# Attention prologue: the first head's operands are loaded twice and cast in place, the second head's are split on GpSimd

## The chip, the cores and the metric

One core of a Trainium2 chip runs the whole kernel. TensorE (PE) multiplies, VectorE (DVE), ScalarE (ACT) and GpSimd (POOL) work on elements, SyncE (SP) issues most DMAs. The metric is the device time of one execution in microseconds, the median of several runs; lower is better.

## The reference

The input has B = 2 batches of 8 heads, S = 768 positions, D = 64. The attention is clustered: a query sees a key only where both have the same nearest centroid of 16.

```python
q_assign = np.argmax(np.einsum('bhsd,hcd->bhsc', q_n, c_n), axis=-1)
k_assign = np.argmax(np.einsum('bhsd,hcd->bhsc', k_n, c_n), axis=-1)
mask = q_assign[:, :, :, None] == k_assign[:, :, None, :]
scores = np.where(mask, scale * np.matmul(q, k.transpose(0, 1, 3, 2)), -1e9)
attn = softmax(scores)          # over the keys
x = np.matmul(attn, v)          # then heads side by side: 1536 x 512
h = x @ w_in;  x = (h * sigmoid(h)) @ w_out
x = (sigmoid(x @ w_gate) * (x @ w_val)) @ w_out2
```

## The kernel before

Heads are worked on in pairs: a pair p has two heads j = 0 and 1, whose 64 features lie in partitions 0 to 63 (L) and 64 to 127 (U) of the tiles qq and kk. There are eight pairs, and each has 12 tiles of 128 queries (6 for each head). A tile takes scores (TensorE, L467), a row maximum (VectorE, L475), the exponential (ScalarE, L480), transposes of it (L495, L506) and, every third tile, the product with the values (L514). After the eight pairs come the two MLPs, which this change does not touch.

Scores are kept to float32 accuracy by splitting q and k into a high part in the short type fp32r and the rest. The operand qa of head j holds the high part of q in one half of the partitions and the low part in the other; ka holds the high part of k in both halves; qm and km hold the high q against the low k in one half and, in the other, 16 mask rows, one for each cluster. A mask row of a query is -2^100 at all clusters but its own, so that keys of other clusters drop out.

To find the clusters, product_of_clusters (L151) multiplies the centroids cc with qq and kk, scaled (L276) multiplies by one over each centroid's norm, similarities (L164) transposes the result so that positions lie in partitions, ranked (L169) finds the best centroid, and first_choice (L310) makes one-hot rows oh. choice_rows (L323) transposes these back, and query_rows (L326) and key_rows (L334) write them into qm and km.

For pairs 1 to 7 this is prep (L382): GpSimd scales qq in place and makes the splits, and SyncE copies the halves inside SBUF (L402 to L407), then the mask rows (L454, L455). Pieces of it are put between the tiles of the pair before (PIECES, L642). With pair 1 the cluster products come in the fourth tile of pair 0; they use the scaled qq.

Pair 0 has its own code, the prologue, from L186 to L617. In it the order on TensorE, VectorE, ScalarE and SyncE is the order in which the code is written; only GpSimd's is left to the planner, which goes by its own estimate of times, under the constraints issue_after. qq and kk are loaded in one DMA each (L199, L200); ScalarE and VectorE make the splits of both heads at once (L283 to L286); SyncE then copies halves with nine DMAs (L289 to L294) and loads vv (L295); load(1) (L133) brings qq, kk and vv of pair 1, whose qq and kk share their buffers with those of pair 0. warm(n) puts n products of a zero tile on TensorE as fillers; WARM = (10, 1, 8, 5) counts them: before the cluster products, behind them, behind the similarities, and at the end. GpSimd zeroes the unused halves of qm, km and oh (zeros, L236), for pair 1 behind `late` (L358), the low part of the second head's k.

After the prologue only TensorE's order is fixed by hand (steady, L667), until the MLPs, which again fix only TensorE's. ring (L486 in the old code's tile pool, tag "ph") holds the transposed exponentials and is idle until the first transposes.

Of the kernel before, what the change touches and what calls it, by code (L numbers as in the profile page):

```python
# [10 lines left out]
F32 = mybir.dt.float32  # L11
# [3 lines left out]
AF = mybir.ActivationFunctionType  # L15
# [11 lines left out]
SIGN = -0x80000000  # L27
WARM = (10, 1, 8, 5)


@with_exitstack
def clustered_attention_then_two_mlps(ctx, tc, qT, kT, v, cen, cenT, w1i, w1o, w2g, w2v, w2o, out):
    nc = tc.nc
    B, HP, _, S = qT.shape
    D = cen.shape[2]
    H = 2 * HP
    C = cenT.shape[3]
    P = 128
# [23 lines left out]
    def cast(eng, o, i):  # L62
        if eng is nc.scalar:
            return nc.scalar.activation(o, i, AF.Copy)  # L64
        if eng is nc.gpsimd:
            return nc.gpsimd.tensor_scalar(o, i, 1.0, 1.0, op0=ALU.mult, op1=ALU.mult)
        return nc.vector.tensor_copy(o, i)  # L67
# [41 lines left out]
    with ExitStack() as att:  # L109
# [40 lines left out]

        def product_of_clusters(pm, p, q, k):  # L151

            for h in range(2):
                for n, t in enumerate((q, k)):
                    r = slice(32 * (2 * h + n), 32 * (2 * h + n + 1))
                    nc.tensor.matmul(
                        pm[r, 0:HS].rearrange("p (i c) -> p i c", c=P),
                        lhsT=cc[:, p % HP].rearrange("p j c -> p (j c)"),
                        rhs=t.rearrange("p (i h c) -> p h i c", h=2, c=P)[:, h],
                        start=True,  # L160
                        stop=True,
                    )
# [30 lines left out]
        nc.vector.memset(cc, 0.0)  # L193
        for j, r in enumerate((L, U)):
            act_dma(cc[r, :, j], cenT[j])
        qq = raw.tile([P, S], F32, tag="qq", name="qq0")
        kk = raw.tile([P, S], F32, tag="kk", name="kk0")
        vv = hd[0].tile([P, 2, NT, D], F32, tag="vv", name="vv0")
        dma(qq, qT[0, 0])  # L199
        dma(kk, kT[0, 0])  # L200

# [62 lines left out]
        unit = cp.tile([P, HP], F32, tag="unit", name="unit")  # L264
        nc.vector.tensor_reduce(n2, csq, axis=AX.X, op=ALU.add)
        nc.scalar.activation(identb, ident, AF.Copy)
        nc.scalar.activation(r0, n2, AF.Sqrt)
# [14 lines left out]
        qh, ql, kh = (st.tile([P, S], R32, tag=t, name=f"{t}0") for t in ("qh", "ql", "kh"))  # L282
        nc.scalar.activation(qh, qq, AF.Copy, scale=scale)  # L283
        nc.vector.scalar_tensor_tensor(ql, qq, scale, qh, op0=ALU.mult, op1=ALU.subtract)
        cast(nc.scalar, kh, kk)
        nc.vector.tensor_tensor(km[L, 0], kk[L], kh[L], op=ALU.subtract)  # L286

        for j, (r, o) in enumerate(((L, U), (U, L))):
            dma(qa[r, j].bitcast(F32), qh[r].bitcast(F32))  # L289
            dma(ka[L, j].bitcast(F32), kh[r].bitcast(F32))  # L290
            dma(ka[U, j].bitcast(F32), kh[r].bitcast(F32))
            dma(qa[o, j].bitcast(F32), ql[r].bitcast(F32))
            if j:
                dma(qm[r, j].bitcast(F32), qh[r].bitcast(F32))  # L294
        dma(vv, v[0, 0])  # L295

        pm = ps_s.tile([P, 512], F32, tag="s", name="pm0")
        product_of_clusters(pm, 0, qq, kk)
        warm(WARM[1])
        sim = wk.tile([P, NT, 2, 2, C], F32, tag="sim", name="sim0", bufs=1)  # L300
        sums = sim.rearrange("p t n j c -> p (t n j c)")
        scaled(0, sums, pm[:, 0:HS])
        nc.scalar.activation(qm[L, 0], qq[L], AF.Copy, scale=scale)
        ps = ps_t.tile([P, 512], F32, tag="t", name="ps0")
        similarities(ps, sums)
        warm(WARM[2])

        chosen = []

        def first_choice(j, seen):  # L310
            sg = seen.rearrange("p (w j c) -> p j w c", j=2, c=C)[:, j]
            wq, mw = yield from ranked(0, j, sg, 2 * NT)
            if j == 0:
                chosen.append(mw)
            for n in range(2):
# [34 lines left out]
        for _ in first_choice(0, ps[:, 0:HS]):  # L350
            pass
        cast(nc.scalar, sums, ps[:, 0:HS])
        ex = sm.tile([P, 1], F32, tag="ex", name="ex", bufs=1)
        nc.scalar.activation(ex, unit[:, 0:1], AF.Exp)
        mine = sm.tile([P, 2 * NT], F32, tag="mine", name="mine", bufs=1)
        with tc.issue_after(cast(nc.gpsimd, mine, chosen.pop()).ins):
            with tc.issue_after(zeros(0, 1).ins):
                late = nc.gpsimd.tensor_tensor(km[U, 1], kk[U], kh[U], op=ALU.subtract)  # L358
        half = NT // 2
        pts = [ps_t.tile([P, 1024], BF16, tag="t", name=f"pt0_0{n}") for n in range(2)]  # L360
        choice_rows(pts[1], 0, 0, half)
        for n in range(2):
            for i in range(half):
                choice_rows(pts[n], 0, n * half + i, i)
        query_rows(0, pts[1], half, 0, 1)
        chosen.append(key_rows(nc.vector, 0, pts[0], 0, 0, half))
        key_rows(nc.scalar, 0, pts[1], 0, half, half)
        query_rows(0, pts[0], 1, 1, half - 1)
        query_rows(0, pts[1], 0, half, half)

        on_pool = {}
# [113 lines left out]

        ring = wk.tile([P, NT, S], F32, tag="ph", name="ph", bufs=1)  # L486
        shared = {}
# [655 lines left out]
def _layout(i):  # L1143
# [10 lines left out]
    def columns(w):  # L1154
# [12 lines left out]
        "cen": np.broadcast_to(cen.transpose(1, 2, 0, 3), (2, 2, *cen.shape[1:3], H // 2, D)).reshape(P, H // 2, D),  # L1167
        "cenT": cen.transpose(1, 3, 0, 2),
        "w1i": columns(i["moe_w_in"]),
# [25 lines left out]
```

## Time and profile before

| | |
|---|---|
| median of 3 runs | 775.22 us (774.85 to 776.21) |
| the profiled execution | 775.89 us, of which the span from the first to the last instruction is 774.2 |
| TensorE busy | 761.2 us (98%) |
| VectorE, ScalarE, GpSimd busy | 623.7, 403.1, 393.4 us |
| DMA | 71.60 MB, mean 92 GB/s |

Busy time of TensorE counts a product until its modelled end, so it is a share of time in which products were under way, not of what the array can do. Times in the rows below are us from the start of the span.

### The profile page before, as it was taken

How to read it: one execution, taken by the hardware profiler on the slowest of the kernel's cores; microseconds unless marked ns; L12 is line 12 of the kernel's file. 1: busy time of each engine (PE TensorE's matmuls, PEld its weight loads, DVE VectorE, ACT ScalarE, POOL GpSimd, SP SyncE). 2: the span in 40 equal slices, each digit the busy share in tenths (PEclk: the TensorE clock that was granted, in tenths of full speed). 3: DMA queues.
4: the chain of work that ended last, by engine and by line, in shares of the span. 5: the costliest groups of instructions: out<-in, count | busy, mean ns of one | idle time of the engine just before them, and what ended most of it. 6: DMA issues, size and time to landing. Idle time of an engine off the chain costs nothing.

```text
span 774.2 us, 11459 instructions
## 1 busy us (share of the span) xinstructions
PE 761.2 (98%) x4313; PEld 652.5 (84%) x4314; DVE 623.7 (81%) x787; ACT 403.1 (52%) x691; POOL 393.4 (51%) x345
## 2 busy tenths in 40 slices
PE   7999999999999999999999999999999999999998
PEld 4666776677768998898989989998998989899896
DVE  7887887788797968989779669997596997979645
ACT  6777776776886662533615526546442425343120
POOL 5334134643655773755647515544573837748320
PEclk9999999999999999999999999999999999999999
DMA  7776457447122122233122111221121221121004
GB/s 214 183 198 172 113 153 194 116 126 200 35 85 70 58 82 83 82 112 100 36 80 83 54 55 55 88 78 55 36 73 55 82 83 55 55 82 55 1 0 163
DMA packets 25487, 71.60 MB, mean 92 GB/s; under 512 B 4484, under 2 KB 4952, under 8 KB 25432
## 3 DMA queue, kind: packets, MB, share of 16 engines
q1 hardware_dynamic: 24888, 70.84, 31.0%
q8 instruction: 34, 0.56, 0.3%
q14 instruction: 21, 0.17, 0.1%
q10 hardware_dynamic: 544, 0.03, 0.0%
HBM read 48.01 MB, written 3.19 MB: 66 GB/s over the span
## 4 chain that ended last, share of the span: by engine, by line
PE 86%; DVE 8%; DMA 2%; issue 1%; ACT 1%; SPq 0%; ACTq 0%; DVEq 0%
PE z L1012 12%; PE s L467 7%; PE v L514 7%; PE t L506 5%; PE y L953 4%; PE h_0w L837 3%; PE h_0x L837 3%; PE g_0w L837 3%; PE u L495 2%; PE g_0x L837 2%; PE v_0w L837 2%; PE v_0x L837 2%; PE r L903 2%; PE q L903 2%; PE y_20None L953 2%; PE y_11None L953 2%
## 5 line engine op out<-in xcount | busy, mean ns | idle before, releaser
L480 ACT ACTIVATE e<-s,nm 128x768 f32<-128x768 f32 x96 | 86.4, 900 | 26.7 <-DVE nm L475 26.5
L475 DVE TENSOR_REDUCE nm<-s 128x1 f32<-128x768 f32 x96 | 91.4, 953 | 10.8 <-PE s L467 9.8
L1012 PE MATMUL z<-wu,ghb 128*128 128x512 f32 (+1 forms) x292 | 89.6, 388 | 0.5 <-DVE acc L933 0.5
L514 PE MATMUL v<-ph,vv 128*64 128x384 f32 x384 | 69.2, 494 | 0.2 <-DVE ph L67 0.2
L1012 PEld LDWEIGHTS z<-wu,ghb 128*128 128x128 f32 x292 | 54.1, 188 | 12.5 <-issue 1.3
L467 PE MATMUL s<-ka,qa 128*128 128x384 f32 x192 | 57.7, 381 | 2.3 <-ACT e L480 1.9
L506 PE MATMUL t<-ident,e 128*128 128x128 f32 x384 | 58.4, 275 | 1.4 <-ACT ph L64 0.5
L1012 PE MATMUL z<-wu,glb 128*128 128x512 f32 (+1 forms) x146 | 57.0, 391 | 0.0
L514 PEld LDWEIGHTS v<-ph,vv 128*64 128x64 f32 x384 | 25.2, 136 | 32.8 <-issue 28.5
L64 ACT ACTIVATE ph<-t 128x512 f32<-128x512 f32 x68 | 40.6, 598 | 23.1 <-PE t L506 22.3
L467 PE MATMUL s<-k,q 128*128 128x384 f32 x192 | 49.6, 339 | 0.8 <-DMA q<-rows 0.8
L506 PEld LDWEIGHTS t<-ident,e 128*128 128x128 f32 x384 | 44.1, 140 | 4.5 <-DVE ph L67 3.6
L933 DVE TENSOR_TENSOR acc<-z,acc 128x1024 f32<-128x1024 f32 (+2 forms) x32 | 36.6, 1153 | 13.6 <-PE z L1012 13.0
L67 DVE COPY ph<-u 128x512 f32<-128x512 f32 x48 | 32.8, 683 | 18.1 <-PE u L495 18.1
L545 POOL TENSOR_TENSOR acc<-xf,rb 128x768 f32<-128x768 f32 x7 | 12.8, 1834 | 61.2 <-DMA rb<-d_rb 49.2
L495 PEld LDWEIGHTS u<-ident,e 128*128 128x128 f32 x192 | 23.4, 141 | 21.4 <-issue 18.6
L495 PE MATMUL u<-ident,e 128*128 128x128 f32 x192 | 38.5, 282 | 0.0
L734 POOL TENSOR_TENSOR wo<-co,wo 128x512 fp32r<-128x512 f32 x16 | 22.5, 1410 | 30.0 <-ACT wo L64 30.0
L467 PEld LDWEIGHTS s<-k,q 128*128 128x128 f32 x192 | 34.6, 188 | 1.3 <-DMA q<-rows 1.1
L467 PEld LDWEIGHTS s<-ka,qa 128*128 128x128 f32 x192 | 28.9, 190 | 5.5 <-ACT e L480 3.4
L1012 PEld LDWEIGHTS z<-wu,glb 128*128 128x128 f32 x146 | 27.4, 188 | 7.1 <-DVE glb L893 1.6
L953 PE MATMUL y<-gha,wo 128*128 128x384 f32 x128 | 32.8, 334 | 0.0
(627 smaller groups left out, 2125.4 us busy)
## 6 DMA issues: line engine op xcount, KB each, us to landing
ri<-in_w1i SPq DMA_DIRECT2D x16, 512.0 KB, 3.3
ro<-in_w1o SPq DMA_DIRECT2D x16, 512.0 KB, 3.3
ka<-kh SPq DMA_DIRECT2D x32, 192.0 KB, 3.6
rg<-in_w2g SPq DMA_DIRECT2D x12, 512.0 KB, 3.2
rv<-in_w2v SPq DMA_DIRECT2D x12, 512.0 KB, 3.3
ru<-in_w2o SPq DMA_DIRECT2D x12, 512.0 KB, 3.3
qq<-in_qT SPq DMA_DIRECT2D x8, 384.0 KB, 4.2
kk<-in_kT SPq DMA_DIRECT2D x8, 384.0 KB, 4.2
```

The costliest lines, as they stand in the source:

```text
L64: return nc.scalar.activation(o, i, AF.Copy)
L67: return nc.vector.tensor_copy(o, i)
L467: nc.tensor.matmul(s[:, g, 0:HS], lhsT=a[:, j, i * P : (i + 1) * P], rhs=c[:, j, g * HS : (g + 1) * HS], start=n == 0, stop=n == 1,)
L475: maxima.append(nc.vector.tensor_reduce(nm, s[:, :, 0:HS], axis=AX.XY, op=ALU.max, negate=True))
L480: x = nc.scalar.activation(e, s[:, :, 0:HS], AF.Exp, bias=nm, scale=1.0, accum_out=tots[p][:, n : n + 1])
L495: nc.tensor.transpose(both[:, kt - 4, i % 2, :], e[:, kt * P : (kt + 1) * P], ident)
L506: nc.tensor.transpose(t[:, kt, :], e[:, kt * P : (kt + 1) * P], ident)
L514: m = nc.tensor.matmul(o[(L, U)[kt % 2]], lhsT=vv[:, j, kt, :], rhs=ring[:, kt, g * G : (g + 1) * G], start=n < 2, stop=n >= NT - 2,)
L837: nc.tensor.matmul(o[:, b, 0:HS], lhsT=w[a][s][:, k, :], rhs=right[b, q][t][:, k, :], start=start and k == 0 and n == 0, stop=k == KQ - 1 ...
L933: nc.vector.tensor_tensor(z, o, z, op=ALU.add)
L953: nc.tensor.matmul(o[:, d, 0:width], lhsT=s[:, d, k, :], rhs=t[:, c], start=k == 0 and m == 0, stop=k == 1 and m == 2,)
L1012: nc.tensor.matmul(o[:, a, c], lhsT=s[:, q * P : (q + 1) * P], rhs=r[:, c], start=k == 0 and m == 0, stop=k == 1 and m == 2, skip_group_ch ...
```

## The change

The first head's rows (partitions 0 to 63 of the DRAM arrays) are loaded twice, into both halves of two slices of ring, sq0 and sk0. Casts from there write qa, ka, qm and km of head 0 where they are used, so that no DMA copies them. The second head's rows are loaded into the upper halves of qq and kk. Cluster products of head 0 use 64 rows of sq0 and sk0; head 1 has its own products, transposes and sums behind those. GpSimd scales qq[U] in place and makes kh, qh and ql of head 1, and SyncE copies these with five DMAs, issued behind the first choice. The centroids for cc come in one DMA, from which VectorE makes two copies. The ScalarE table for the exponential is loaded earlier. The fillers are 7, 1, 7 and 5.

```diff
@@ -25,7 +25,7 @@
 
 LARGEST = 122879.9921875 * 2.0**-112
 SIGN = -0x80000000
-WARM = (10, 1, 8, 5)
+WARM = (7, 1, 7, 5)
 
 
 @with_exitstack
@@ -34,7 +34,7 @@
     B, HP, _, S = qT.shape
     D = cen.shape[2]
     H = 2 * HP
-    C = cenT.shape[3]
+    C = cenT.shape[2]
     P = 128
     NT = S // P
     HS = S // 2
@@ -148,15 +148,15 @@
         heads = {}
         L, U = slice(0, D), slice(D, P)
 
-        def product_of_clusters(pm, p, q, k):
+        def product_of_clusters(pm, p, q, k, rows=slice(0, P)):
 
             for h in range(2):
                 for n, t in enumerate((q, k)):
                     r = slice(32 * (2 * h + n), 32 * (2 * h + n + 1))
                     nc.tensor.matmul(
                         pm[r, 0:HS].rearrange("p (i c) -> p i c", c=P),
-                        lhsT=cc[:, p % HP].rearrange("p j c -> p (j c)"),
-                        rhs=t.rearrange("p (i h c) -> p h i c", h=2, c=P)[:, h],
+                        lhsT=cc[rows, p % HP].rearrange("p j c -> p (j c)"),
+                        rhs=t[rows].rearrange("p (i h c) -> p h i c", h=2, c=P)[:, h],
                         start=True,
                         stop=True,
                     )
@@ -191,13 +191,18 @@
         dma(cr, cen)
         cc = cp.tile([P, HP, 2, C], F32, tag="cc", name="cc")
         nc.vector.memset(cc, 0.0)
-        for j, r in enumerate((L, U)):
-            act_dma(cc[r, :, j], cenT[j])
+        ct = cp.tile([P, HP, C], F32, tag="ct", name="ct")
+        act_dma(ct, cenT)
+        ring = wk.tile([P, NT, S], F32, tag="ph", name="ph", bufs=1)
+        staged = ring[:, 0], ring[:, 1]
+        for r in (L, U):
+            for t, a in zip(staged, (qT, kT)):
+                dma(t[r], a[0, 0][L])
         qq = raw.tile([P, S], F32, tag="qq", name="qq0")
         kk = raw.tile([P, S], F32, tag="kk", name="kk0")
         vv = hd[0].tile([P, 2, NT, D], F32, tag="vv", name="vv0")
-        dma(qq, qT[0, 0])
-        dma(kk, kT[0, 0])
+        for t, a in zip((qq, kk), (qT, kT)):
+            dma(t[U], a[0, 0][U])
 
 
         wt = fin.tile([P, S], F32, tag="rb", name="wt").bitcast(BF16)[:, 0:512]
@@ -263,6 +268,8 @@
         n2, r0, r1, r2, r3, r4 = (norm(f"r{n}") for n in range(6))
         unit = cp.tile([P, HP], F32, tag="unit", name="unit")
         nc.vector.tensor_reduce(n2, csq, axis=AX.X, op=ALU.add)
+        for j, r in enumerate((L, U)):
+            nc.vector.tensor_copy(cc[r, :, j], ct[r])
         nc.scalar.activation(identb, ident, AF.Copy)
         nc.scalar.activation(r0, n2, AF.Sqrt)
         nc.vector.tensor_scalar_max(r1, r0, 1e-30)
@@ -280,38 +287,34 @@
         qm, km = q2[0], k2[0]
         heads[0] = (qa, qm, ka, km, vv)
         qh, ql, kh = (st.tile([P, S], R32, tag=t, name=f"{t}0") for t in ("qh", "ql", "kh"))
-        nc.scalar.activation(qh, qq, AF.Copy, scale=scale)
-        nc.vector.scalar_tensor_tensor(ql, qq, scale, qh, op0=ALU.mult, op1=ALU.subtract)
-        cast(nc.scalar, kh, kk)
-        nc.vector.tensor_tensor(km[L, 0], kk[L], kh[L], op=ALU.subtract)
-
-        for j, (r, o) in enumerate(((L, U), (U, L))):
-            dma(qa[r, j].bitcast(F32), qh[r].bitcast(F32))
-            dma(ka[L, j].bitcast(F32), kh[r].bitcast(F32))
-            dma(ka[U, j].bitcast(F32), kh[r].bitcast(F32))
-            dma(qa[o, j].bitcast(F32), ql[r].bitcast(F32))
-            if j:
-                dma(qm[r, j].bitcast(F32), qh[r].bitcast(F32))
-        dma(vv, v[0, 0])
-
+        sq0, sk0 = staged
+        cast(nc.scalar, ka[L, 0], sk0[L])
+        nc.gpsimd.tensor_scalar(qm[L, 0], sq0[L], scale, 1.0, op0=ALU.mult, op1=ALU.mult)
         pm = ps_s.tile([P, 512], F32, tag="s", name="pm0")
-        product_of_clusters(pm, 0, qq, kk)
+        product_of_clusters(pm, 0, sq0, sk0, L)
         warm(WARM[1])
+        nc.vector.tensor_tensor(km[L, 0], sk0[L], ka[L, 0].bitcast(F32), op=ALU.subtract)
         sim = wk.tile([P, NT, 2, 2, C], F32, tag="sim", name="sim0", bufs=1)
         sums = sim.rearrange("p t n j c -> p (t n j c)")
         scaled(0, sums, pm[:, 0:HS])
-        nc.scalar.activation(qm[L, 0], qq[L], AF.Copy, scale=scale)
         ps = ps_t.tile([P, 512], F32, tag="t", name="ps0")
         similarities(ps, sums)
+        nc.scalar.activation(qa[:, 0], sq0, AF.Copy, scale=scale)
+        cast(nc.scalar, ka[U, 0], sk0[U])
+        pm = ps_s.tile([P, 512], F32, tag="s", name="pm0_1")
+        product_of_clusters(pm, 0, qq, kk, U)
         warm(WARM[2])
+        nc.gpsimd.tensor_scalar(qq[U], qq[U], scale, 1.0, op0=ALU.mult, op1=ALU.mult)
+        cast(nc.gpsimd, kh[U], kk[U])
+        cast(nc.gpsimd, qh[U], qq[U])
+        ex = sm.tile([P, 1], F32, tag="ex", name="ex", bufs=1)
+        nc.scalar.activation(ex, unit[:, 0:1], AF.Exp)
 
         chosen = []
 
         def first_choice(j, seen):
             sg = seen.rearrange("p (w j c) -> p j w c", j=2, c=C)[:, j]
             wq, mw = yield from ranked(0, j, sg, 2 * NT)
-            if j == 0:
-                chosen.append(mw)
             for n in range(2):
                 nc.vector.tensor_tensor(
                     oh[0][:, :, j, n, 0:C],
@@ -349,24 +352,36 @@
 
         for _ in first_choice(0, ps[:, 0:HS]):
             pass
-        cast(nc.scalar, sums, ps[:, 0:HS])
-        ex = sm.tile([P, 1], F32, tag="ex", name="ex", bufs=1)
-        nc.scalar.activation(ex, unit[:, 0:1], AF.Exp)
-        mine = sm.tile([P, 2 * NT], F32, tag="mine", name="mine", bufs=1)
-        with tc.issue_after(cast(nc.gpsimd, mine, chosen.pop()).ins):
-            with tc.issue_after(zeros(0, 1).ins):
-                late = nc.gpsimd.tensor_tensor(km[U, 1], kk[U], kh[U], op=ALU.subtract)
+        scaled(0, sums, pm[:, 0:HS])
+        lows = nc.vector.scalar_tensor_tensor(
+            qa[U, 0], sq0[U], scale, qa[U, 0].bitcast(F32), op0=ALU.mult, op1=ALU.subtract
+        )
+        with tc.issue_after(lows.ins):
+            lows = nc.gpsimd.tensor_tensor(ql[U], qq[U], qh[U], op=ALU.subtract)
+        dma(qa[U, 1].bitcast(F32), qh[U].bitcast(F32))
+        dma(ka[L, 1].bitcast(F32), kh[U].bitcast(F32))
+        dma(ka[U, 1].bitcast(F32), kh[U].bitcast(F32))
+        dma(qm[U, 1].bitcast(F32), qh[U].bitcast(F32))
+        dma(qa[L, 1].bitcast(F32), ql[U].bitcast(F32))
+        dma(vv, v[0, 0])
+        with tc.issue_after(lows.ins):
+            last = zeros(0, 1)
+        with tc.issue_after(last.ins):
+            late = nc.gpsimd.tensor_tensor(km[U, 1], kk[U], kh[U], op=ALU.subtract)
         half = NT // 2
         pts = [ps_t.tile([P, 1024], BF16, tag="t", name=f"pt0_0{n}") for n in range(2)]
         choice_rows(pts[1], 0, 0, half)
         for n in range(2):
             for i in range(half):
                 choice_rows(pts[n], 0, n * half + i, i)
+        ps = ps_t.tile([P, 512], F32, tag="t", name="ps0_1")
+        similarities(ps, sums)
         query_rows(0, pts[1], half, 0, 1)
         chosen.append(key_rows(nc.vector, 0, pts[0], 0, 0, half))
         key_rows(nc.scalar, 0, pts[1], 0, half, half)
         query_rows(0, pts[0], 1, 1, half - 1)
         query_rows(0, pts[1], 0, half, half)
+        cast(nc.scalar, sums, ps[:, 0:HS])
 
         on_pool = {}
 
@@ -483,7 +498,6 @@
             latest[:] = [x]
             prob[p, j, i] = e
 
-        ring = wk.tile([P, NT, S], F32, tag="ph", name="ph", bufs=1)
         shared = {}
 
         def transposes(p, j, i):
@@ -1165,7 +1179,7 @@
         "kT": pairs(k),
         "v": v.reshape(B, H // 2, 2, S // P, P, D).transpose(0, 1, 4, 2, 3, 5),
         "cen": np.broadcast_to(cen.transpose(1, 2, 0, 3), (2, 2, *cen.shape[1:3], H // 2, D)).reshape(P, H // 2, D),
-        "cenT": cen.transpose(1, 3, 0, 2),
+        "cenT": cen.transpose(1, 3, 0, 2).reshape(P, H // 2, -1),
         "w1i": columns(i["moe_w_in"]),
         "w1o": w1o.reshape(K // P // 2, M // P // 2, P, -1),
         "w2g": columns(i["moe2_w_gate"]),
```

## Rows read from the trace of the kernel before

**Rows 1.** TensorE's waits in the whole kernel: us in total, times, longest.
```profile
PE s L467 <- DMA q<-rows: 0.8, 1, 0.8
```

**Rows 2.** Timeline of TensorE, first 21 us: start, us, engine, line, operation.
```profile
3.86 0.15 PEld L209 LDWEIGHTS <-wt 128*128 128x128 bf16 x1 [0.28 <-issue]
4.29 0.15 PEld L209 LDWEIGHTS <-wt 128*128 128x128 bf16 x1 [0.28 <-issue]
...
5.95 0.48 PE L156 MATMUL pm<-qq,cc 128*32 128x384 f32 x1 [0.75 <-DMA cc<-in_cenT]
...
6.32 0.49 PE L156 MATMUL pm<-kk,cc 128*32 128x384 f32 x1
...
7.97 1.89 PE L209 MATMUL pw<-wt 128*128 128x512 bf16 x8
10.31 0.55 PE L324 MATMUL pt<-identb,oh 128*64 128x128 bf16 x7 [0.45 <-DVE oh L316]
...
20.65 0.48 PE L156 MATMUL pm<-qq,cc 128*32 128x384 f32 x1
```

**Rows 3.** Timeline of ScalarE in the prologue.
```profile
5.68 0.84 ACT L64 ACTIVATE kh<-kk 128x768 fp32r<-128x768 f32 x1 [0.55 <-DMA kk<-in_kT]
6.89 0.58 ACT L276 ACTIVATE sim<-pm,unit 128x384 f32<-128x384 f32 x1 [0.36 <-PE pm L156]
7.37 0.83 ACT L303 ACTIVATE q<-qq 64x768 fp32r<-64x768 f32 x1
...
9.54 1.28 ACT L354 ACT_TABLE_LOAD   x1
10.83 0.20 ACT L354 ACTIVATE ex<-unit 128x1 f32<-128x1 f32 x1
...
11.35 0.48 ACT L337 ACTIVATE k<-pt 16x384 fp32r<-16x384 bf16 x1
```

**Rows 4.** Timeline of VectorE in the prologue.
```profile
5.18 0.18 DVE L273 RECIPROCAL unit<-r 128x4 f32<-128x4 f32 x1
...
8.17 0.36 DVE L172 TENSOR_REDUCE mx<-ps 128x12 f32<-128x192 f32 x1 [0.66 <-PE ps L167]
...
9.70 0.46 DVE L316 TENSOR_TENSOR oh<-wq,mw 128x96 bf16<-128x96 bf16 x2
```

**Rows 5.** Timeline of SyncE's DMA issues: first copy, load of pair 1's kk.
```profile
5.16 0.55 SPq L289 DMA_DIRECT2D qa<-qh  x1
...
14.77 0.33 SPq L138 DMA_DIRECT2D kk<-in_kT  x1
```

**Rows 6.** Timeline of GpSimd: late, and pair 1's first operation.
```profile
11.31 1.83 POOL L358 TENSOR_TENSOR k<-kk,kh 64x768 fp32r<-64x768 f32 x1
...
19.30 0.84 POOL L394 TENSOR_SCALAR qq<-qq 128x768 f32<-128x768 f32 x1 [2.65 <-DMA qq<-in_qT]
```

**Rows 7.** Windows of the prologue; last column GB/s of all DMA.
```profile
2.00:5.00 3.00, 3.00 (x9) 0.98 (x7) 1.66 (x8) 2.49 (x5) 1.54 (x3) 1.00 0.97 306
5.50:6.00 0.50, 0.05 (x4) 0.08 (x8) 0.50 (x1) 0.32 (x1) 0.00 (x0) 1.00 0.00 0
6.00:7.50 1.50, 1.12 (x9) 0.20 (x9) 1.18 (x2) 1.14 (x3) 0.00 (x0) 1.00 0.58 131
7.50:14.50 7.00, 5.59 (x31) 3.28 (x32) 4.44 (x12) 5.30 (x11) 4.73 (x6) 1.00 0.96 217
14.50:19.50 5.00, 4.79 (x35) 4.07 (x36) 4.64 (x10) 3.58 (x8) 2.30 (x4) 1.00 0.94 304
```

**Rows 8.** Windows while two rows are broadcast from DRAM into 64 partitions each.
```profile
82.86:83.86 1.00, 1.00 (x8) 0.29 (x4) 0.93 (x3) 1.00 (x4) 0.00 (x0) 1.00 0.71 258
165.05:166.05 1.00, 1.00 (x8) 0.46 (x10) 0.97 (x2) 0.95 (x2) 0.00 (x0) 1.00 0.64 218
```

**Rows 9.** Chain of waits: pair 1's mask rows.
```profile
33.29 3.88 DMA q<-rows
```

**Rows 10.** DMA issues of the whole kernel: KB each, median us to landing.
```profile
q<-rows SPq DMA_DIRECT2D x14, 48.0 KB, 2.1
```

## The prediction

> **What bounds the kernel now.** I read the page's busy shares first, then TensorE's waits, then each engine's timeline over the first 22 us, then the DMA rates by stretch. TensorE is busy nearly all the time, so a change outside its own work can only move the moments at which it stands still. After the first tiles there is one such moment of size, 0.8 us before pair 1's first masked scores, for mask rows that come by DMA [rows 1]. The rest of the change's reach is the start. There the reader should see this chain: filler products, the cluster products at 5.95 behind a DMA (cc, though kk had landed at about 5.66), the similarities, eight fillers, the choice rows at 10.31 [rows 2]. ScalarE, with kk at 5.68, the scaled sums at 6.89 and the last key rows from 11.35 to 11.83, lets the first masked score go [rows 3]. VectorE ranks from 8.17 and has the one-hot rows at 10.16 [rows 4]. From then on the tiles run one behind another until the cluster products of pair 1 at 20.65 [rows 2].
>
> Behind this runs a second chain, easily overlooked. SyncE copies head halves in SBUF and then loads pair 1's qq and kk [rows 5]. GpSimd has zeroed all its buffers by 16.65 (19.30 less its idle 2.65) and waits until 19.30 for that qq [rows 6]. Pair 1's cluster products need GpSimd's scaled qq, so TensorE follows it with 0.51 us to spare (19.30 + 0.84 = 20.14 against 20.65). So a faster start is worth only as much as pair 1's load lets through.
>
> **First loads.** Six half loads of 197 KB (192 KiB) take the place of two of 393 KB: 1180 KB against 786 KB. Loads into 128 partitions ran at 306 GB/s; copies between 64-partition halves at 217 GB/s [rows 7]. The nearest rows to a DRAM load into 64 partitions are the later broadcasts into halves: 258 GB/s in the first microsecond, 218 in the poorest [rows 8]. I take 260, with 306 and 217 as the ends. In the sum, T is the landing of the last half, kk[U]. The old kk landed at 5.66; 786 KB at 306 GB/s is 2.57 us and 1180 KB at 260 is 4.54, so T = 5.66 - 2.57 + 4.54 = 7.63 (6.95 at 306; 8.53 at 217). The first two halves land 393/260 = 1.51 us into the same stretch, at 4.60 (4.38 to 4.90).
>
> [...]
>
> **First head, first choice.** The small cc transfers shrink to one and two VectorE copies, which I put at 0.3 us on the six small operations that end with unit at 5.36, so unit at 5.7 [rows 4]. Cluster products take 0.86 us (5.95 to 6.81), on 64 rows as on 128, since the columns are the same [rows 2]; casts likewise cost 0.83 against 0.84 us for half or all partitions [rows 3]. Products 4.65 to 5.5; scaled (0.58) to 6.3; similarities and lags as before (ranking started 0.70 us after scaled ended): ranking at 7.0; one-hot rows 1.99 us later, at 9.0 [rows 3, 4]. That is 1.2 us earlier. The km subtraction lies between unit and the ranking.
>
> **The fillers and second product take this back.** In TensorE's order the choice rows now stand behind the second head's products and seven fillers. That is T + 0.05 + 0.86 + 0.05 + 7 x 0.236 (1.89/8 [rows 2]) = T + 2.6 = 10.23, later than the one-hot rows. ScalarE is not later: 6.3, two casts of 0.84, a table load of 1.28 with a small operation of 0.2, scaled again 0.58, ends at 10.05. The old choice rows stood at 10.31, so the first masked score moves by only -0.1 us (-0.8 at 306, +0.8 at 217). The four copies that the first scores stood behind are gone; their wait lay under this chain, so it gives nothing more.
>
> **Second head on GpSimd.** qq[U] is scaled in place, so that it waits for the second product (T + 0.9). kh[U] can run in its shadow. Then scale and qh, 0.83 each: T + 2.58. SyncE's five copies stand behind qh, the first in line; vv and pair 1's loads stand behind them all. Data moved about 0.85 us after an issue (issued at 5.16, nothing until 6.0, 131 GB/s to 7.5 [rows 5, 7]). Five copies of 197 KB at 217 GB/s take 4.53: done at T + 7.98 = 15.61. The nine old ones were done at about 14.75 (1.5 us at 131 and 7 us at 217 GB/s are 1716 of their 1769 KB). So fewer copies, started later, end 0.86 us later (0.2 to 1.8), and vv and qq behind them land as much later: qq at 20.15. GpSimd is not the later one: ql 1.83, two memsets 1.4 (five took 13.14 to 16.65), late 1.83, five memsets 3.5 end at T + 11.2 = 18.9 [rows 6]. kk waits for late as its buffer's last reader, to about 15.3; it was issued at 14.77 [rows 5] and still stands behind qq's data. If GpSimd instead takes the scale before kh, all this is 0.83 us later.
>
> **The sum.** Pair 1's cluster products: 20.14 + 0.86 = 21.0 against 20.65, +0.35 (-0.3 to +1.3). The twelve copies of pair 1 start 0.86 later. The mask rows for which TensorE waits landed 3.88 us after their issue [rows 9], against a median of 2.1 in the whole kernel [rows 10]: they stood in that queue. So the end follows the queue more than TensorE; between +0.35 and +0.86 I take +0.7. The profiled execution, 775.89 (span 774.2 and 1.7 around it), would become 776.6; it lies 0.67 above the median of the runs, so against 775.22 I forecast **775.9**. All later work on TensorE is unchanged and costs nothing as long as only these waits move.
>
> **Rivals.** A measurement of this kernel tells 0.2%, 1.55 us, from no change.
> - *Halves load at the full 306 GB/s.* T = 6.95; the start gains 0.8, but the copies still end 0.2 later; the end moves by -0.3 to +0.2: 775.1. For it: 306 in the first stretch; against: 218 to 258 in rows 8. Chance 0.2.
> - *Halves at 217, or GpSimd scales before it casts.* The end moves by +1.2 to +1.8, 776.7, half of this above the bound. For it: the copies' rate [rows 7]; GpSimd's order here is the planner's. Chance 0.2. Both together, +2.4 (777.6): 0.05.
> - *Slower, by TensorE's clock.* [...] If the slow level lasted until past 10 us, the second product would cost 0.86 and the fillers 1.35 more, so choice rows at 12.4, and the kernel +2.0: 777.2. It decides only when it holds for most of the seven fillers; a delay to 8 us costs 0.4. Against it: the products from 5.95 and the gap of 0.75 before them went at the fast level. Chance 0.05.
> - *Faster.* Pair 1's loads don't hold, and the planner puts the mask rows before other traffic: -0.9 at the start and the 0.8 wait gone, -1.7: 773.5. Rows 9 and 10 show that the place in the queue matters; nothing shows that it would change. Chance 0.06.
>
> **How the numbers follow.** The likeliest case, 775.4 to 776.3, has 0.44. Low end 774.6: below the full-rate case, leaving out the faster one. High end 777.2: over the 217 rival, leaving out the doubled one and part of the clock's. Faster 0.06. Slower: half of 0.2, 0.05, 0.05, rounded to 0.2. Same 0.74.
>
> **What the profile would show.** Right: cluster products at 4.5 to 4.9, before 5.95; the second head's at 7 to 8.5, and the choice rows directly behind seven fillers, without idle time, near 10.2; VectorE's one-hot rows near 9.0; the first pair 1 qq operation on GpSimd at 19.9 to 20.5; pair 1's cluster products near 21 with an idle stretch before them, and a wait for mask rows of about 0.8 or more. Wrong: choice rows before 9.6 and pair 1's products before 20.0 (a gain not given back); idle time before choice rows (the one-hot rows bind, not the fillers); copies' data before 10.5, which would mean that the queue does not wait for qh as reckoned.

## The result, and the profile after

The changed kernel took 780.64 us (median of 5 runs, 779.32 to 781.27) against 776.21 (774.85 to 776.51) beside it: a ratio of 1.0056 with a 95% interval of 1.0043 to 1.0069. It is slower by 0.56%, where I had forecast no difference (775.9, at most 777.2). The profiled execution took 779.42, span 777.6: +3.4 on the span before. So the profile shows 3.4 of the 4.4 us that lie between the medians. Each ratio below is to the kernel before, run on the same chip.

TensorE's timeline after (start, us, operation; it answers to [rows 2]):

```profile
1.32 3.17 PE L214 MATMUL pw<-wt 128*128 128x512 bf16 x7 [1.32 <-DVE sq L232]
4.78 1.55 PE L156 MATMUL pm<-ph,cc 64*32 64x384 f32 x8 [0.29 <-DMA ph<-in_qT]
6.26 0.39 PE L214 MATMUL pw<-wt 128*128 128x512 bf16 x1
7.11 0.52 PE L167 MATMUL ps<-ident,sim 128*128 128x128 f32 x3 [0.46 <-ACT sim L283]
8.73 0.81 PE L156 MATMUL pm<-qq,cc 64*32 64x384 f32 x1 [1.10 <-DVE wq L177]
9.28 0.85 PE L156 MATMUL pm<-kk,cc 64*32 64x384 f32 x1
...
10.71 3.17 PE L214 MATMUL pw<-wt 128*128 128x512 bf16 x7
13.81 0.96 PE L327 MATMUL pt<-identb,oh 128*64 128x128 bf16 x7
...
24.54 0.48 PE L156 MATMUL pm<-qq,cc 128*32 128x384 f32 x1
```

The first head's products do start 1.2 us earlier than before, and one of them takes 0.48 to 0.60 us, about as before (0.48 to 0.51). But a product of the second head takes 0.81 to 0.85, and the seven fillers behind it take 3.17 us where eight took 1.89. The choice rows come 3.5 us later than before and pair 1's products 3.9 later. The choice rows stand directly behind the fillers, without idle time. The wait of 1.10 names VectorE's wq, which ended at about that time; in two experiments below the same product names the DMA of qq, the half that it reads.

The same stretch in windows (busy time of PE, PEld, DVE, ACT and POOL; then granted TensorE clock, DMA share, GB/s; it answers to [rows 7]):

```profile
2.00:5.00 3.00, 2.71 (x7) 0.78 (x6) 1.92 (x9) 1.05 (x4) 1.81 (x4) 1.00 0.88 220
6.00:7.50 1.50, 1.04 (x8) 0.41 (x4) 0.95 (x1) 1.42 (x3) 0.00 (x0) 1.00 1.04 207
8.50:13.50 5.00, 4.77 (x15) 1.25 (x15) 2.46 (x5) 2.13 (x4) 3.39 (x4) 0.50 0.01 2
13.50:15.00 1.50, 1.50 (x10) 1.02 (x10) 0.52 (x1) 0.14 (x1) 1.44 (x2) 0.50 0.71 160
15.30:20.00 4.70, 4.42 (x27) 3.38 (x26) 3.50 (x6) 3.45 (x9) 4.57 (x6) 1.00 1.01 235
```

Two things are to be seen. The half loads, all into the upper halves in the window from 6.0, run at 207 GB/s, near the rate of the copies in [rows 7] (217), not at 260. And the granted clock is 0.50, the lower of the two levels that these windows show, from 8.50 to 15.0; it is 0.96 between 8.00 and 8.50, so that it fell while TensorE stood idle for 1.10 us (7.63 to 8.73). The column shows 1.00 in the first microseconds too, where the seven fillers start 0.43 us apart; there the level is read from the durations. By these the clock had risen during the first head's products: the filler at 6.26 takes 0.39 and the similarities 0.52, as in the kernel before.

Not every execution went this way. Over the whole execution the mean granted clock was 0.995 and 0.996 in two of the five (779.42 and 781.27 us), and 1.00 in the other three (779.32 to 780.99). As the column reads 1.00 also where the level is low from the start, the record doesn't show what the clock did in those three.

GpSimd and SyncE's issues after ([rows 5, 6]):

```profile
4.72 0.82 POOL L292 TENSOR_SCALAR q<-ph 64x768 fp32r<-64x768 f32 x1 [1.13 <-DMA ph<-in_qT]
9.39 0.93 POOL L66 TENSOR_SCALAR kh<-kk 64x768 fp32r<-64x768 f32 x1 [3.85 <-DMA kk<-in_kT]
...
11.90 0.83 POOL L66 TENSOR_SCALAR qh<-qq 64x768 fp32r<-64x768 f32 x1
...
21.84 0.83 POOL L409 TENSOR_SCALAR qq<-qq 128x768 f32<-128x768 f32 x1 [0.36 <-DMA qq<-in_qT]
```

```profile
4.32 0.60 SPq L205 DMA_DIRECT2D kk<-in_kT  x1
12.76 0.50 SPq L361 DMA_DIRECT2D qa<-qh  x1
```

The last half, kk[U], was issued at 4.32 and landed at 9.22 (its row in the DMA issues has 4.9 us to landing). The copies wait for qh and start at 12.76, so the DMA engines move 2 GB/s from 8.5 to 13.5. TensorE's list of waits after has no row for mask rows any more; the 0.8 us of [rows 1] is gone. Pair 1's mask rows were issued 3.9 us later than before (37.20 against 33.29), as much as TensorE was late. But pair 2's loads, which stand ahead of them, were issued only 3.1 later (33.73 against 30.65), and the first rows then took 2.5 us to land, not 3.88 [rows 9].

### The profile page after: what moved, and what is told of

It is laid out like the page before. It is cut to its first block, busy times and chain, and to the rows that moved or that the text cites. A ratio compares the mean times of both kernels' runs of the same rounds, so it can differ in the third digit from the quotient of the medians.

```text
span 777.6 us, 11483 instructions
## 1 busy us (share of the span) xinstructions
PE 765.9 (98%) x4321; PEld 653.6 (84%) x4321; DVE 625.0 (80%) x789; ACT 404.0 (52%) x692; POOL 399.9 (51%) x349
## 4 chain that ended last, share of the span: by engine, by line
PE 86%; DVE 9%; issue 1%; DMA 1%; ACT 1%; POOL 0%; SPq 0%; ACTq 0%; DVEq 0%
PE z L1026 12%; PE s L482 8%; PE v L528 8%; PE t L520 5%; PE y L967 4%; PE h_0w L851 3%; PE h_0x L851 3%; PE u L509 3%; PE g_0w L851 2%; PE g_0x L851 2%; PE v_0w L851 2%; PE v_0x L851 2%; PE r L917 2%; PE q L917 2%; PE y_20None L967 2%; PE y_11None L967 2%
```

## The experiments

**Fillers before the second products, and seven fillers in the kernel before.** My first theory was that the clock, which fell after 1.10 us of idle time, made the loss, and that the place of the fillers decides it. The rival: the late second half decides.

```diff
e1_fill, on the changed kernel:
         cast(nc.scalar, ka[U, 0], sk0[U])
+        warm(7)
         pm = ps_s.tile([P, 512], F32, tag="s", name="pm0_1")
e2_before7, on the kernel before:
-WARM = (10, 1, 8, 5)
+WARM = (7, 1, 7, 5)
```

> The changed kernel with seven more fillers between the similarities of head 0 and the second head's products, so that TensorE is not idle from 7.6 to 8.7 us. If the fall of the granted clock to half (8.5 to 15.3 us) is what the late choice rows cost, and the idle stretch brings it on: the clock stays at 1.00, the second products take 0.86 us instead of 2.05 and the next seven fillers 1.65 instead of 3.1, choice rows near 11.9 instead of 13.8, and the kernel about 2 us faster than the changed one, near 778.5. If the late landing of the last half load is all that matters: choice rows at 13.5 or later and no change of time.

> The kernel before with the fillers of the change, 7, 1, 7 and 5, and nothing else. If the number of fillers at the start alone lets the clock fall: granted clock 0.50 somewhere between 5 and 15 us and 2 us or more slower. If it takes the idle stretch behind the similarities, which this kernel doesn't have: clock 1.00, choice rows at 10.3, and no difference (within 0.2%).

e1_fill: ratio 1.0064 (1.0044 to 1.0084), no better than the change. e2_before7: 1.0009 (1.0000 to 1.0018). The fillers of e1_fill, and then of e2_before7, in TensorE's timeline:

```profile
8.68 3.19 PE L214 MATMUL pw<-wt 128*128 128x512 bf16 x7
...
12.89 1.68 PE L214 MATMUL pw<-wt 128*128 128x512 bf16 x7
```

```profile
6.12 0.82 PE L156 MATMUL pm<-qq,cc 128*32 128x384 f32 x1 [1.64 <-DMA cc<-in_cenT]
...
9.11 2.39 PE L209 MATMUL pw<-wt 128*128 128x512 bf16 x7
11.49 0.55 PE L324 MATMUL pt<-identb,oh 128*64 128x128 bf16 x7
```

The cure missed: the low level held from the start until 12.3, so the new fillers only put the products off. In this execution the first head's products already took 0.82 to 0.85 us each, although the code up to them is the changed kernel's. So it does not test whether filling the gap keeps a level that has been reached. What both profiles show is that with seven fillers at the start the engine had not reached the fast level at the first products (0.82 us each instead of 0.48), in the kernel before too. In e2_before7 the choice rows came 1.2 us later than before, and the kernel lost no more than 0.2%: there is slack of about the 0.8 us for which TensorE waited anyway, and that wait is gone from its list.

**Ten and eight fillers; the second head's halves loaded earlier.**

```diff
e4_after10, on the changed kernel:
-WARM = (7, 1, 7, 5)
+WARM = (10, 1, 8, 5)
e3_order, on the changed kernel: q[U], k[U] before the upper copies
-        for r in (L, U):
-            for t, a in zip(staged, (qT, kT)):
-                dma(t[r], a[0, 0][L])
+        for t, a in zip(staged, (qT, kT)):
+            dma(t[L], a[0, 0][L])
...
+        for t, a in zip(staged, (qT, kT)):
+            dma(t[U], a[0, 0][L])
```

> The changed kernel with the fillers of the kernel before, 10, 1, 8 and 5. If the shorter first run of fillers lets the clock fall: it stays at 1.00, choice rows near 12.1 (one filler more), and 2 us faster than the changed kernel. If the idle stretch from 7.6 to 8.7 does: the clock falls at about the same time, choice rows near 14.2, and no faster than the changed kernel.

> The changed kernel with the upper halves of qq and kk loaded before the upper copies of the first head, same bytes, same fillers. If the order of the half loads sets when TensorE goes on: kk's half lands near 7.4 instead of 9.2, the second products start near 7.6 without the idle 1.1 us and at full clock, and choice rows stand near 10.2; ScalarE, which now waits for the copies (near 8.3 and 9.2), writes the last key rows near 12.9, so about 1 us slower than the kernel before. If the clock falls whatever the gap is: choice rows at 12 or later and 3 us slower than the kernel before.

e3_order: 1.0054 (1.0040 to 1.0069). GpSimd has kk[U] at 7.40 instead of 9.39, yet the low level lasts until about 13.2, the second products take 8.47 to 9.97 and the seven fillers 3.17: choice rows at 13.01. e4_after10: 1.0044 (1.0031 to 1.0057), which overlaps the changed kernel's interval; the timeline tells more. Its TensorE:

```profile
9.80 1.90 PE L214 MATMUL pw<-wt 128*128 128x512 bf16 x8
11.63 0.58 PE L327 MATMUL pt<-identb,oh 128*64 128x128 bf16 x7
...
20.09 0.61 PE L482 MATMUL s<-ka,qa 128*128 128x384 f32 x2 [1.15 <-ACT e L495]
...
23.29 0.48 PE L156 MATMUL pm<-qq,cc 128*32 128x384 f32 x1
```

The choice rows are 2.2 us earlier than in the changed kernel, with one filler more: the clock had cost about that much (kk[U] came 0.25 us earlier here). But pair 1's products are only 1.25 earlier, because of a new wait of 1.15. It goes back to VectorE (first fence), which compares beside GpSimd's `late` (second):

```profile
16.17 1.68 DVE L175 TENSOR_TENSOR eq<-sim,mx 128x192 bf16<-128x192 f32 x1
```

```profile
15.80 1.83 POOL L370 TENSOR_TENSOR k<-kk,kh 64x768 fp32r<-64x768 f32 x1
```

The comparison takes 0.36 us elsewhere, as in the kernel before at 14.48. It ends at 17.85, just after `late` (17.63).

**Half loads in the kernel before.** If loading by halves is what is slow, it must cost the kernel before too, with the same bytes.

```diff
e5_halves, on the kernel before:
-        dma(qq, qT[0, 0])
-        dma(kk, kT[0, 0])
+        for r in (L, U):
+            for t, a in zip((qq, kk), (qT, kT)):
+                dma(t[r], a[0, 0][r])
```

> The kernel before with pair 0's qq and kk loaded in four halves of 64 partitions in the order lower, lower, upper, upper; nothing else. If a load into one half runs at about 209 GB/s like the copies: kk whole near 6.9 instead of 5.66, cluster products near 7 instead of 5.95, choice rows 1.0 to 1.2 later, and about 1 us slower. If halves load at 306 GB/s: products at 6.0 and no difference.

1.0029 (1.0019 to 1.0039), 2.1 us, twice what I had expected. ScalarE has qq at 6.57 instead of 4.29, and TensorE kk at 7.44 instead of by 5.95:

```profile
6.62 0.80 PE L156 MATMUL pm<-qq,cc 128*32 128x384 f32 x2 [1.01 <-DMA qq<-in_qT]
7.44 0.48 PE L156 MATMUL pm<-kk,cc 128*32 128x384 f32 x1
```

From 3 to 5 us the DMA engines moved 259 GB/s (263, 255) where the kernel before moves 327 (325, 329); the expectation had 209 or 306. Pair 1's products stand at 22.50, 1.85 us later than before. So half loads cost this kernel 0.3% by themselves, with all its fillers and no GpSimd splits.

**`late` before the memsets; the half loads alternated.**

```diff
e6_late, on e4_after10:
         with tc.issue_after(lows.ins):
-            last = zeros(0, 1)
-        with tc.issue_after(last.ins):
             late = nc.gpsimd.tensor_tensor(km[U, 1], kk[U], kh[U], op=ALU.subtract)
+        with tc.issue_after(late.ins):
+            last = zeros(0, 1)
...
-        with tc.issue_after(late.ins):
+        with tc.issue_after(last.ins):
             zeros(1, 0)
e8_alt, on e4_after10:
-        for r in (L, U):
-            for t, a in zip(staged, (qT, kT)):
-                dma(t[r], a[0, 0][L])
...
-        for t, a in zip((qq, kk), (qT, kT)):
-            dma(t[U], a[0, 0][U])
+        for t, u, a in zip(staged, (qq, kk), (qT, kT)):
+            dma(t[L], a[0, 0][L])
+            dma(u[U], a[0, 0][U])
+        for t, a in zip(staged, (qT, kT)):
+            dma(t[U], a[0, 0][L])
```

> The changed kernel with 10, 1, 8 and 5 fillers, and the operation late on GpSimd ahead of the two memsets that stood before it, so that it no longer runs when VectorE compares sim with mx for the second head. If VectorE and GpSimd shut each other out while both read SBUF: that comparison takes 0.36 instead of 1.68 us, the tiles behind it come 1.3 us earlier, pair 1's products near 22.0 instead of 23.3, and the kernel is about 1.3 us faster than with the fillers alone (779.6), near 778.4. If the long comparison had another cause: it stays at 1.6 or more and the time at 779.6.

> The changed kernel with 10, 1, 8 and 5 fillers and the half loads in turn, lower and upper: sq0, qq, sk0, kk, then the two upper copies. If two halves together use what one alone leaves idle: near 260 GB/s or more over the first four, kk's half landed before 7.5 instead of 9.1; choice rows near 10.8 and 0.5 to 1 us faster than with the fillers alone, since ScalarE then waits for the copies. If the rate belongs to 192 KB transfers and not to the half: about 209 GB/s as before and kk's half at 7.5 or later only by its place.

e6_late: 1.0049 (1.0038 to 1.0061), no gain. The comparison falls to 0.55 us and TensorE's wait from 1.15 to 0.28, and then pair 1's products wait 0.53 us for GpSimd's scaled qq, whose load had ended 0.19 us after GpSimd was free, and then for the load of kk (the weight load, PEld, names it):

```profile
22.73 0.83 PE L156 MATMUL pm<-qq,cc 128*32 128x384 f32 x2 [0.53 <-POOL qq L409]
23.54 0.11 PEld L156 LDWEIGHTS pm<-kk,cc 128*32 128x32 f32 x1 [0.68 <-DMA kk<-in_kT]
23.55 0.51 PE L156 MATMUL pm<-kk,cc 128*32 128x384 f32 x1
```

So the comparison and the load queue are two bounds close behind one another. e8_alt: 1.0034 (1.0021 to 1.0046); kk[U] is there at 7.48, the choice rows at 11.11, but the comparison again takes 1.68 and pair 1's products start at 22.84. Its interval overlaps that of e4_after10. The gain in kk[U] is one of order: from 4 to 7 us the stream moved 241 GB/s (240, 261, 221) against 223 (209, 255, 206) in the changed kernel, far from 327. Three other profiles with the changed kernel's order of loads have 214 (e6_late), 224 (e1_fill) and 233 (e4_after10), so that alternating gave between 3 and 13%.

**Whole loads, both products together.** Whole loads of qq and kk, the two extra halves behind them, both heads' products at once, `late` first.

```diff
e7_full, on the changed kernel (the core; head 0 then takes qq[L], kk[L] for sq0[L], sk0[L]):
-WARM = (7, 1, 7, 5)
+WARM = (10, 1, 8, 5)
...
+            dma(t, a[0, 0])
+        for t, a in zip(staged, (qT, kT)):
+            dma(t[U], a[0, 0][L])
...
+        product_of_clusters(pm, 0, qq, kk, L)
+        product_of_clusters(pm1, 0, qq, kk, U)
```

> The changed kernel repaired in three places: qq and kk loaded whole first, and after them only the upper copies of the first head; both heads' products one behind the other before the similarities; 10, 1, 8 and 5 fillers and late ahead of the memsets. If half loads, idle TensorE and the shared reading are the causes: products near 5.8, choice rows near 10.4, copies of head 1 issued near 9.5, pair 1's products near 20.7, and the time within 0.15% of the kernel before. If casting in place and splitting on GpSimd cost something by themselves: 1.5 us or more slower than the kernel before.

1.0088 (1.0072 to 1.0104), the slowest of all, though both products were done at 7.96. So the second branch came: casting in place and splitting on GpSimd cost something by themselves. VectorE, GpSimd, TensorE and the windows:

```profile
11.11 1.40 DVE L319 TENSOR_TENSOR oh<-wq,mw 128x96 bf16<-128x96 bf16 x1
12.43 1.85 DVE L319 TENSOR_TENSOR oh<-wq,mw 128x96 bf16<-128x96 bf16 x1
```

```profile
10.59 1.80 POOL L360 TENSOR_TENSOR ql<-qq,qh 64x768 fp32r<-64x768 f32 x1
12.35 1.82 POOL L368 TENSOR_TENSOR k<-kk,kh 64x768 fp32r<-64x768 f32 x1
```

```profile
14.43 0.92 PE L327 MATMUL pt<-identb,oh 128*64 128x128 bf16 x7 [3.47 <-DVE oh L319]
```

```profile
14.00:20.00 6.00, 5.32 (x21) 4.30 (x23) 3.93 (x6) 3.19 (x8) 5.19 (x9) 0.50 0.96 277
20.00:21.00 1.00, 1.00 (x7) 0.76 (x5) 0.93 (x3) 0.77 (x2) 0.72 (x1) 0.92 0.87 347
```

Two one-hot operations that take 0.46 us together [rows 4] took 3.18, beside two GpSimd subtractions that ran back to back: the first ended at 12.51, just after the first subtraction (12.39), the second at 14.28, just after the second (14.17). TensorE then stood idle for 3.47 us, and its granted clock was 0.50 for the next six.

**The queue, both bounds, and the kernel before's own queue.**

```diff
e9_vv, on e8_alt: vv behind the half loads instead of behind the five copies
+        dma(vv, v[0, 0])
...
-        dma(vv, v[0, 0])
e10_both: e9_vv, with the edit of e6_late
e11_order, on the kernel before:
-        dma(vv, v[0, 0])
...
             load(1)
+            dma(vv, v[0, 0])
```

> The changed kernel with 10 and 8 fillers and the half loads alternated between the two halves of the partitions (e8_alt), and the first head pair's values vv issued straight behind the half loads instead of behind the five copies, in the time in which the DMA engines stood idle (0 GB/s from 8.5 to 13.5 us). If pair 1's loads bind, through the queue behind the copies: pair 1's kk lands about 1.3 us earlier, pair 1's cluster products stand near 21.7 instead of 22.84, and the kernel is about 1 us faster than e8_alt, +0.2% on the kernel before. If VectorE's long comparison (1.68 us at 16.17) and TensorE's own chain bind: the products stay near 22.8 and the ratio near e8_alt's +0.34%.

> e9_vv, and late (the low part of the second head's k on GpSimd) put ahead of the memsets, so that it does not run beside VectorE's comparison of pair 0. If the two are two bounds one behind the other (comparison, then loads), the comparison takes 0.6 us or less, the loads of pair 1 are early too, its cluster products stand near 21.3, and the kernel comes to within 0.15% of the kernel before. If only the queue mattered: the same as e9_vv.

> The kernel before with one edit: the load of vv is issued behind pair 1's qq and kk instead of ahead of them. If pair 1's place in the queue sets the end of the prologue, as I wrote in the prediction, pair 1's qq is scaled by GpSimd about 1.3 us earlier (near 18.0 instead of 19.30), the mask rows leave earlier and the 0.8 us wait for them shrinks: up to 0.8 us (0.1%) faster. If the queue does not bind the kernel before: no change within 0.1%, with pair 1's products still near 20.65.

e9_vv: 1.0026 (1.0016 to 1.0036). Pair 1's scale on GpSimd waits for no load, as already in e8_alt, and pair 1's products still start at 22.98: the comparison took 1.69. e10_both: 1.0022 (1.0012 to 1.0032). The comparison takes 0.36, pair 1's products start at 21.87 straight behind the scores, and GpSimd works without a pause into pair 1. VectorE and TensorE of e9_vv, then of e10_both:

```profile
15.86 1.69 DVE L175 TENSOR_TENSOR eq<-sim,mx 128x192 bf16<-128x192 f32 x1
22.98 0.48 PE L156 MATMUL pm<-qq,cc 128*32 128x384 f32 x1
```

```profile
15.80 0.36 DVE L175 TENSOR_TENSOR eq<-sim,mx 128x192 bf16<-128x192 f32 x1
21.87 0.48 PE L156 MATMUL pm<-qq,cc 128*32 128x384 f32 x1
```

In the profiles, then, `late` alone (e6_late) or the loads alone (e8_alt, e9_vv) left pair 1's products at 22.7 to 23.0, and only both brought them to 21.87. The times tell less: e9_vv and e10_both each lie below the changed kernel's interval, but e8_alt, e9_vv and e10_both overlap one another, so that neither what vv's place adds to the alternated loads nor what `late` adds to both is shown in time. e10_both did not come within 0.15%: of the expectation, the mechanism holds in the profile and the size does not. e11_order: 1.0002 (0.9994 to 1.0011). GpSimd has pair 1's qq at 18.33 instead of 19.30 and the wait for mask rows is gone, but in this execution cc came 0.7 us later [rows 2], about as much as the wait, and pair 1's products stood at 21.95. No difference can be told.

**The table load earlier.**

```diff
e12_table, on e10_both:
         nc.vector.reciprocal(unit, r4)
+        ex = sm.tile([P, 1], F32, tag="ex", name="ex", bufs=1)
+        nc.scalar.activation(ex, unit[:, 0:1], AF.Exp)
...
-        ex = sm.tile([P, 1], F32, tag="ex", name="ex", bufs=1)
-        nc.scalar.activation(ex, unit[:, 0:1], AF.Exp)
```

> e10_both, and the small exponential that loads ScalarE's table moved from between the casts of the first head and the scaled sums of the second (10.26 to 11.75 us in e10_both) to right behind the norms, where ScalarE stands idle from 4.17 to 6.29. In e10_both ScalarE lets the first masked scores go at 13.01. If what is left of the loss (+0.22%) is TensorE's chain through ScalarE, the first masked scores come at 11.8 to 12.4, pair 1's cluster products near 21.4, and the ratio falls to about +0.15%. If GpSimd, which has no idle time left ahead of pair 1's scale at 20.65, holds the rest, the scores come earlier but pair 1's products stay above 21.4 and the ratio near +0.2%.

1.0036 (1.0022 to 1.0049): a miss. ScalarE's wait goes, but the first masked scores only move from 13.01 to 12.96, now behind VectorE: the low part of qa takes 1.47 us beside a cast and a 2.41 us subtraction on GpSimd (0.96 beside a memset, in e7_full), then the key rows end at 12.81. Pair 1's products start at 21.90, as in e10_both. Most of the 2.1 us by which the span of this profile exceeds that of e10_both (776.8 against 774.7) comes later, in code that no edit touched. VectorE, GpSimd and TensorE:

```profile
50.17 2.06 DVE L436 TENSOR_TENSOR wq<-eq,mk 128x384 bf16<-128x384 bf16 x1
```

```profile
49.71 2.10 POOL L414 TENSOR_TENSOR kl<-kk,kh 128x768 fp32r<-128x768 f32 x1
```

```profile
54.46 0.66 PE L520 MATMUL t<-ident,e 128*128 128x128 f32 x4 [1.43 <-DVE ph L67]
```

The same operation, wq, takes 0.54 in e10_both and 1.04 in the kernel before. In e10_both it ran beside a cast on GpSimd (50.42 to 51.68); in the kernel before it began beside a cast that ended at 50.26, and a subtraction followed at 50.34; in e12_table it began 0.46 us behind the subtraction above and ended at 52.23, 0.42 after it. So in these three profiles its time went with where it fell against GpSimd's operations.

## Why the prediction was wrong

Two terms of the sum failed: T, the landing of the last half, and the price of the second product and its fillers, for which I took the fast level of the clock.

**First loads: mis-sized.** T was 9.22, not 7.63. By the sum's own working, 1180 KB in 9.22 - 3.09 us (5.66 - 2.57) are 192 GB/s, below even the 217 end (the bytes themselves ran at 206 to 255 a microsecond from 4 to 7, and stopped about 1 us before the landing). The 306 for whole loads was low too; from 3 to 5 us they ran at 327. The rows chosen, broadcasts from DRAM, were the wrong neighbours; the SBUF copies, also 192 KB into 64 partitions, were the right ones, and e5_halves shows the price alone. The bytes themselves moved faster than 192: the sum counts the time from the last byte to the landing as transfer.

**The fillers and second product: right in form, 3.6 us short.** I had the choice rows at T + 2.6 = 10.23; they came at 13.81. Of the 3.58, T made 1.59. The rest is the clock: from the last half to the products' end 1.55 (9.22 to 10.77) instead of 0.91, and from there 3.04 instead of 1.70, together 1.98.

**The clock rival: its price near, its chance wrong.** At the choice rows I had reckoned 2.2 us for it: 0.86 for the second product once more, and 1.35 for seven fillers at the 0.43 us between the first ones (3.86, 4.29) instead of 0.236 [rows 2]. The profile shows 1.98; in time it was not isolated, since e4_after10 overlaps the change. I gave +2.0 us and 0.05. What I held against it, that products from 5.95 ran fast, was seen behind ten fillers and says nothing of seven; e2_before7 shows the kernel before slow at that very place (0.82 us a product at 6.12, against 0.48). The way was another than I wrote: in the profiled execution the level had been reached and fell in the gap before the late half, while in e1_fill and e3_order it had not been reached. And I priced it against T = 7.63: late loads and a low clock at once, which happened, were not added up.

**VectorE beside GpSimd: left out.** The change moves five operations to GpSimd, and I asked only when GpSimd would be done with them. VectorE operations beside them grew: unit came at 5.97 instead of 5.7 because one operation on 128x4 took 0.72 us instead of 0.16 from 4.84 on, beside GpSimd's from 4.72; the low part of qa took 1.47. In the changed kernel itself this stayed off the path (ScalarE waited 3.36 us for the choice rows); with a faster start it became the bound, as the profiles of e4_after10 and e7_full show. The comparison eq took 1.68 us beside `late` in e4_after10, and 0.36 in e10_both, where `late` had been moved. Why the two did not run side by side, no run isolates.

**ScalarE not later: right.** Its second scaled sums ended at 11.51, and it then waited for TensorE.

**Second head on GpSimd and the queue: order right, not the bound.** kh did run before the scale, and the copies stood behind qh. qq's scale came at 21.84, not 20.15, and pair 1's products at 24.54, not 21.0; but those started straight behind TensorE's scores. "The end follows the queue more than TensorE" was wrong: the end moved +3.4 with TensorE's +3.9, less the 0.8 us wait, which did not grow but went. Of the queue it was right that the mask rows' landing follows what stands ahead of them: with 0.8 us more between pair 2's loads and them (3.9 against 3.1), the first took 2.5 us to land, not 3.88. Pair 1's loads were the next bound behind TensorE (e6_late).

**What stays open.** With fillers, order of loads, vv and `late` mended, e10_both is still 0.22% above the kernel before, and no version beat that kernel. Its profile is one of its fastest executions (776.51, median 777.58), with a span of 774.7, only 0.5 above. So most of what is left lies in executions that were not profiled. The record points at two things. One is the collision of e12_table, which is not the change's alone: e5_halves, the kernel before but for its loads, has it in its profile, beside a GpSimd subtraction of 2.09 us. The granted clock was 0.50 from 57 to 59 us, and that execution, 781.06, is the slowest of twelve. VectorE and TensorE of e5_halves:

```profile
51.99 2.05 DVE L422 TENSOR_TENSOR wq<-eq,mk 128x384 bf16<-128x384 bf16 x1
56.28 0.95 PE L507 MATMUL t<-ident,e 128*128 128x128 f32 x4 [1.98 <-DVE ph L67]
```

The other is the clock. In e8_alt the two executions with a mean granted clock of 0.998 took 780.9 and 781.2 us, the other seven, at 0.999 and 1.00, took 777.66 to 778.62. In e10_both the two slowest, 779.96 and 779.99, have 0.998 and 0.996, and the other ten 0.999 or 1.00. Where the clock fell in them, and whether a collision came before, is not shown.

## What to carry to other kernels

When a change loads by halves of the partitions, take the price from a transfer of that shape, and add up the mishaps that can come together: a late load and a slow TensorE clock came at once here, and each added its own cost (1.59 and 1.98 us at the choice rows). Fillers are part of the path's timing, so a level of the clock seen behind ten of them is no evidence for seven. Before moving elementwise work to GpSimd, list the VectorE operations that will run beside it, and allow for a wait like the one here: a comparison of 0.36 us took 1.68, and ended 0.22 us after the GpSimd subtraction beside it (e4_after10). And when executions of one kernel differ, look at the granted clock of each before trusting one profile.

## What the runs showed of the hardware

- In e7_full two one-hot operations of VectorE took 1.40 and 1.85 us instead of 0.46 together, beside two GpSimd subtractions of 1.80 and 1.82, and each ended about 0.1 us after one of these.
- Two operations on 128x4 were longer beside a GpSimd operation: one with two inputs (0.72 us instead of 0.16, at 4.84 in the changed kernel) and one with a single tensor input (0.78 instead of 0.17, at 5.02 in e4_after10). GpSimd was longer too: a cast of 0.83 took 1.46 in e8_alt at 7.48, beside a two-input subtraction of VectorE from 7.28.
- Behind 1.10 us of idle time in the changed kernel the granted clock was 0.50 for 6.5 us, with TensorE busy in 6.27 of them. It was 0.50 also behind 1.98 us (e5_halves) and 3.47 us (e7_full). Behind 1.00 us (e6_late, where the next eight fillers took 1.90) and 1.43 us (e12_table, at 54.46) it stayed at the fast level. Ten fillers at the start do not settle it: in four of the six executions of e6_late the mean granted clock was 0.996 to 0.998.
